# Old state in halves of 64 rows, keys' transposes behind the values' products: a scan of 12 chunks and the two layers behind it

## The chip, the cores and the metric

The kernel runs on one core of a Trainium2 chip. The metric is the device time of one execution in microseconds (us), from the median of several executions. The engines are named as in the profile: PE (TensorE, with PEld for its weight loads), DVE (VectorE), ACT (ScalarE), POOL (GpSimd) and SP, which issues most DMAs.

## The reference, cut to what matters

Three parts run one after the other. The first is a recurrence with a decay w for each head and channel; the second a mixing layer over tokens and then channels; the third sends each token to one of eight experts.

```python
for t in range(S):                                  # S = 768, 8 heads of 48 channels, 2 batches
    cur = einsum('bhd,bhe->bhde', u * kt, vt)
    y[:, :, t] = einsum('bhd,bhde->bhe', rt, state + cur)
    state = w * state + einsum('bhd,bhe->bhde', kt, vt)
x  = y                                              # (2, 768, 384)
u_ = x + (relu(x.T @ w_tok1) @ w_tok2).T            # token mixing
x2 = u_ + relu(u_ @ w_ch1) @ w_ch2                  # channel mixing
...
out[b, s] = p[e] * (relu(x2[b, s] @ w1[e]) @ w2[e]) # e: argmax of x2 @ w_gate, or the token before's
```

## The kernel before, in words

**The scan.** The recurrence is computed in chunks of 128 tokens: 6 chunks for each of 2 batches, so `t` counts 12 chunks. The loop `for t in range(NT)` in `_emit` is one step for each chunk, software-pipelined by hand: step t finishes chunk t and prepares chunks t+1 and t+2. The order of every engine's work is the order in which the code emits it; there is no scheduler. A step emits, for PE: `old(t+1)` (a product with the identity that puts the old state `st` into the PSUM tile `kp`), `scores(t+1)` (keys by queries into two tiles `at`), `pre_ks(t+2)` (four transposes of the scaled keys into `kt`), `beta(t+1)` and `update(t+1)` (both into `kp`), `values(t)` (old state by queries, L431, and masked scores by values, L436, into `y`), `turn(t-1)` (transposes of the result x into `tp`) and products of the token mixing (`mix1`, `mix2`, lines 357 to 359). For DVE: `pre_rk(t+2)` (L372, scales queries and keys by powers of w), `masks(t+1)` (L418), `pre_beta(t+2)` (L377), pieces of the weights' conversion, and `finish(t)`, which reads `y` and writes x (L485). For ACT: the copy of the transposed keys to `ks` (L385), `state(t+1)` (L476, four activations that read `kp` and write the next `st`), the copies of `beta`, eight activations for `bon` (L394), casts and the copies of `tp` (L501). For the first chunk of a batch there is no old state and DVE writes the new one (L480); the last chunk of a batch (t = 5 and 11) needs neither update nor transposed keys. So there are 8 calls of `old` with work in them and 8 of the four activations.

`kp` holds, for two heads at a time, a 128 x 96 block of which only the two 64 x 48 blocks on the diagonal mean anything: rows 0 to 63 with columns 0 to 47, and rows 64 to 127 with columns 48 to 95. The state tiles `sts` are zero elsewhere.

**PSUM tiles in turn.** `ps_tile` hands out five PSUM tiles in turn (`turn_of`, counted by `nps`); whoever gets one must wait until the readers of its last user are done. In the channel mixing's first quarter three of them are accumulators, and two are taken in turn for the products `c1`; behind that, `turn_of` goes back to five.

**Weights' conversion.** The weights arrive as 64-bit numbers. `conv_parts` turns them into a high and a low part in 16 pieces, three calls a piece: DVE scales and masks (L323, L324), joins (L328), joins (L330) and ACT loads the next piece; at the first call of the next piece ACT casts the high part (L291) and POOL subtracts to get the low part (L292). The calls are spread by hand: `CONV_N` in the scan, `CONV_B` in the stretch behind it, and then one list entry of `later` for each `chan_step` of the channel mixing (`work`). A `chan_step(n, f)` is the block f (of 12) for quarter n (of 4): products `ch1` into a tile `c`, ACT's `hh` (L362), DVE's `hl` (L363), and two steps later the products `ch2`. The list `order` weaves quarters 0 and 1: ..., (0, 8), (0, 9), (1, 7), (0, 10), (0, 11), ...

Of the kernel before, what the change touches and what calls it, by code (L numbers as in the profile page):

```python
# [14 lines left out]
ACTF = mybir.ActivationFunctionType  # L15
ALU = mybir.AluOpType
# [6 lines left out]
NCH = S // 128  # L23
NT = B * NCH
# [6 lines left out]
WARM = (6, 12, 3)  # L31
T1 = 4
CONV_N = (0, 2, 2, 3, 2, 3, 2, 2, 2, 2, 1, 0)
CONV_B = (0, 1, 0, 0, 0, 1, 1, -1, 0, 0)
HI_MIN, HI_MAX = (float(x) for x in np.array([0x38100000, 0x47EFFFFF], np.int32).view(np.float32))

# [39 lines left out]
def _emit(ctx, tc, a_in, wu, u_row, wt1, wt2, wc1, wc2, wgl, wex, cst_in, cst_a, out):  # L76
    nc = tc.nc
# [36 lines left out]
    turn_of, nps = [0, 1, 2, 3, 4], [0]  # L114

    def ps_tile(name, shape=(128, 512), k=None):
        if k is None:
            k = turn_of[nps[0] % len(turn_of)]
            nps[0] += 1
        return psw.tile(list(shape), F32, tag=f"w{k}", name=name)  # L120
# [4 lines left out]
    def act(shape, dt, name):  # L125
        return apc.tile(shape, dt, tag=name, name=name)
# [4 lines left out]
    def CA(name):  # L131
        a, b = CSTA[name]
        return cta[:, a:b]
# [4 lines left out]
    def load_a(t, part=None):  # L138
        if t not in a_t:
            rk = ap.tile([128, 1024], F32, tag="rk", name=f"rk{t}", bufs=4)  # L140
            v = ap.tile([128, DM], F32, tag="v", name=f"v{t}", bufs=4)
            a_t[t] = (rk, v)
        for p, (dst, c0) in enumerate(zip(a_t[t], (0, 1536))):
            if part is None or p == part:
                nc.sync.dma_start(out=dst, in_=a_in[t, :, c0:c0 + dst.shape[1]])
# [15 lines left out]
    def warm_up(n):  # L161
        for _ in range(n):
            nc.tensor.matmul(warm_ps, lhsT=warm[:, 0:128], rhs=warm[:, 0:384], start=True, stop=True)
# [43 lines left out]
    for g in range(2):  # L207
        ps = slice(64 * g, 64 * g + 64)
        nc.gpsimd.tensor_tensor(out=uw[ps, :, g], in0=wuc[ps, 4:8], in1=pw[ps, 0], op=ALU.mult)
    w128 = act([128, 4], F32, "w128")  # L210
# [56 lines left out]
    def conv_load():  # L267
        n = nload[0]
        if n >= len(conv) or (n >= 10 and not cpool_):
            return  # L270
        nload[0] += 1
        k, h = conv[n]
        src = wt1 if k == 0 else wt2 if k == 1 else None
        if src is None:
            src = (wc1, wc2)[k % 2][(k - 2) // 2]
        if n < 10:
            raw = rawp.tile([128, 768, 2], I32, tag="raw", name="raw")
        else:
            raw = cpool_[0].tile([128, 768, 2], I32, tag=f"e{n - 10}", name="raw")
        src = src.bitcast(I32)  # L280
        if k > 1 and k % 2 == 0:
            src = src.rearrange("p (c n) -> p c n", c=3)[:, :, h * 512:(h + 1) * 512]
            nc.sync.dma_start(out=raw.rearrange("p (c n) t -> p c (n t)", c=3), in_=src)
        else:
            nc.sync.dma_start(out=raw.rearrange("p n t -> p (n t)"), in_=src[:, h * 1536:(h + 1) * 1536])
        conv_raw.append(raw)
# [65 lines left out]
    def conv_do(n=3):  # L352
        for _ in range(n):
            next(conv_work, None)
# [15 lines left out]
    def pre_rk(t):  # L370
        rk = a_t[t][0]
        nc.vector.tensor_tensor(out=rk, in0=rk, in1=PP.rearrange("p a q j -> p (a q j)"), op=ALU.mult)  # L372
# [6 lines left out]
    def pre_ks(t):  # L379
        rk = a_t[t][0]  # L380
        kt = ps_tile("kt")
        for q in range(4):
            nc.tensor.transpose(kt[:, q * 128:(q + 1) * 128], rk[:, 512 + q * 128:512 + (q + 1) * 128], CA("ident"))
        ks_t[t] = ap.tile([128, 512], F32, tag="ks", name="ks")
        nc.scalar.copy(ks_t[t], kt)  # L385
# [3 lines left out]
    def pre_bonus2(t):  # L389
        beta = ap.tile([128, 8], F32, tag="beta", name="beta")  # L390
        (nc.scalar.copy if t % NCH else nc.vector.tensor_copy)(beta, beta_t.pop(t))
        bon = ap.tile([128, 8, D], F32, tag="bon", name="bon")
        for h in range(8):
            nc.scalar.activation(out=bon[:, h], in_=heads(a_t[t][1])[:, h], func=ACTF.Copy, scale=beta[:, h:h + 1])  # L394
        bon_t[t] = bon

    at_t, ks_t = {}, {}
    kp_t = {}
# [40 lines left out]
    sts = [act([128, 4, 96], F32, f"st{j}") for j in range(3)]  # L439


    def old(t):
        kp = ps_tile("kp")
        kp_t[t] = kp[:, 0:384].rearrange("p (q e) -> p q e", q=4)
        beta_t[t] = kp[:, 384:392]
        if t % NCH in range(1, NCH - 1):
            nc.tensor.matmul(kp_t[t], lhsT=CA("ident"), rhs=sts[(t - 1) % 3], start=True, stop=False)

    def beta(t):
        pp = pp_t.pop(t)  # L450
# [8 lines left out]
    def update(t):  # L459
        ks, v = ks_t.pop(t), a_t[t][1]  # L460
        first = t % NCH == 0
        for h in range(8):
            q, g = divmod(h, 2)
            nc.tensor.matmul(
                kp_t[t][64 * g:64 * g + 64, q, 48 * g:48 * g + 48],
                lhsT=ks[:, h * 64:(h + 1) * 64],
                rhs=v[:, h * D:(h + 1) * D],
                start=first,
                stop=first or q == 3,
            )  # L470

    def state(t):
        kpv = kp_t[t]
        if t % NCH > 0:
            for q in range(4):
                nc.scalar.activation(out=sts[t % 3][:, q], in_=kpv[:, q], func=ACTF.Copy, scale=w128[:, q:q + 1])  # L476
            return
        for g in range(2):
            ps, cs = slice(64 * g, 64 * g + 64), slice(48 * g, 48 * g + 48)
            nc.vector.tensor_tensor(out=sts[t % 3][ps, :, cs], in0=kpv[ps, :, cs], in1=w128[ps].unsqueeze(2).to_broadcast([64, 4, 48]), op=ALU.mult)  # L480

    def finish(t):
        b, c = divmod(t, NCH)
# [92 lines left out]
    for t in range(NT):  # L576
        if t + 3 < NT:
            load_a(t + 3, 0)
        if t == 0:
            conv_load()  # L580
            conv_load()
        grow = t + 1 < NT and (t + 1) % NCH < NCH - 1
        if t + 1 < NT:
            old(t + 1)
            scores(t + 1)
            if t == 0:
                warm_up(WARM[2])
        if t + 2 < NT:
            pre_rk(t + 2)
            if (t + 2) % NCH < NCH - 1:  # L590
                pre_ks(t + 2)
        conv_ahead()
        if t + 1 < NT:
            masks(t + 1)
            beta(t + 1)
        if t + 2 < NT:
            pre_beta(t + 2)
        if grow:
            update(t + 1)
            state(t + 1)  # L600
        values(t)
        if t + 1 < NT:
            pre_bonus2(t + 1)
        if t + 3 < NT:
            load_a(t + 3, 1)
        if t < NT - 1:
            conv_do(CONV_N[t])
        finish(t)
        if t == 0:
            conv_abs(0)  # L610
        if t == NT - 1:
            conv_do(CONV_N[t])
        if t >= 7:
            mix2(*m2.pop(0))
        if t == 10:
            usplit(0)
        if t >= 1:
            turn(t - 1)
            m1.append(t - 1)
            if t >= T1:  # L620
                for _ in range(2):
                    if m1:
                        mix1(m1.pop(0))
# [39 lines left out]
    def ch2(n, f, h):  # L663
        b, half = divmod(n, 2)
        ch, cl = W[f"c2{f // 4}"]
        if f == 0:
            if n == 0:
                turn_of[:] = [0, 1]
            ch_acc[n] = [acc_tile(c) if n else ps_tile("acc", (128, 384), 2 + c) for c in range(3)]
        acc = ch_acc[n]  # L670
        for c in range(3):
            o = (f % 4) * 384 + c * 128
            mm3(acc[c], ch[:, o:o + 128], cl[:, o:o + 128], *h, f == 0, f == 11)
            if f == 11:
                u = xT[b][:, c, half * 384:(half + 1) * 384]
                nc.vector.tensor_tensor(out=u, in0=u, in1=acc[c], op=ALU.add)
        if n == 0 and f == 11:
            turn_of[:] = [0, 1, 2, 3, 4]

    later = []  # L680

# [19 lines left out]

    conv_tail(CONV_B[0])
    turn(11)
    chan_step(0, 0)
    conv_tail(CONV_B[1])
    mix1(11)
    conv_tail(CONV_B[2])
    chan_step(0, 1)
    chan_step(0, 2)
    conv_tail(CONV_B[3])  # L710
    for half in range(2):
        for c in range(3):
            mix2(1, half, c, -1 if half else (2, 0, 1)[c])
            conv_tail(CONV_B[4 + 3 * half + c])
    actx.close()
# [9 lines left out]
    ident = idw[:, 0, 0:128]  # L725
# [493 lines left out]
        for _ in side:  # L1219
            pass  # L1220

    later.extend([lambda j=j: conv_do(2 - j % 2) for j in range(16)])
    later.append(conv_do)
    order = [(0, 3), (1, 0), (1, 1), (1, 2)]
    for f in range(4, 8):
        order += [(0, f), (1, f - 1)]
# [60 lines left out]
    with tc.If(nreg > 0):  # L1287
        with tc.tile_pool(name="ov", bufs=1) as ovp:
# [9 lines left out]
                out=sel, in0=pfx.unsqueeze(1).to_broadcast([128, NOV, 96]), in1=C("ovn").unsqueeze(2).to_broadcast([128, NOV, 96]), op=ALU.is_equal  # L1298
# [91 lines left out]
```

## Time and profile before

| what | before |
|---|---|
| median of 3 executions | 421.62 us (421.58 to 422.22) |
| the profiled execution | 421.5 us, of which 420.0 us are its span |
| PE busy | 397.4 us (95% of the span) |
| DVE, ACT, POOL busy | 274.7, 192.1, 88.4 us |
| granted TensorE clock, mean | 0.987 of full speed |

The scan's loop ends near 100 us; the rest of the token mixing, the channel mixing and the experts follow. The profile's busy share is an average over stages, so the stages are looked at one by one below; a wait is told in brackets behind an instruction, with the engine and line that ended it.

### The profile page before, as it was taken

The numbers are of one execution on the slowest core, as the hardware profiler recorded it, in microseconds if no ns is written. First come the engines' busy times: TensorE is split into PE (matmuls) and PEld (weight loads), VectorE is DVE, ScalarE is ACT, GpSimd is POOL, SyncE is SP. The second block draws the span as 40 slices with busy tenths as digits, with TensorE's granted clock in tenths as the row PEclk, the third lists the DMA queues.
The fourth block names the chain that finished last, engine by engine and source line by source line (L and its number), as shares of the span: only waits on it lengthen the run. The fifth ranks groups of instructions, "written<-read, shape, count | busy, mean of one in ns | idle before, by whom it ended". The sixth has DMA issues, their size and how long they took to land. (4 is left out here: it accounts for less than half of the span.)

```text
span 420.0 us, 8633 instructions
## 1 busy us (share of the span) xinstructions
PE 397.4 (95%) x3348; PEld 378.8 (90%) x3348; DVE 274.7 (65%) x592; ACT 192.1 (46%) x459; POOL 88.4 (21%) x83
## 2 busy tenths in 40 slices
PE   7896987999999998999999999999999999999994
PEld 3685967899999998899999999999999999999994
DVE  6799877775678987447433256759777677675430
ACT  1786566484144333221312121643755665654531
POOL 2016143333122331100000002033241222122110
PEclk9999998999999999999999999999999999999998
DMA  7746462303194000010100013781789867562000
GB/s 259 276 119 224 164 214 90 132 29 108 19 368 159 2 1 0 2 56 2 56 2 1 2 57 104 290 299 28 291 283 419 268 211 247 198 197 89 20 23 14
DMA packets 18336, 55.88 MB, mean 133 GB/s; under 512 B 3921, under 2 KB 7795, under 8 KB 18290
## 3 DMA queue, kind: packets, MB, share of 16 engines
q1 hardware_dynamic: 16370, 49.96, 33.8%
q0 software_dynamic: 1920, 5.32, 4.1%
q8 instruction: 27, 0.44, 0.4%
q14 instruction: 19, 0.16, 0.1%
HBM read 52.31 MB, written 5.91 MB: 139 GB/s over the span
## 5 line engine op out<-in xcount | busy, mean ns | idle before, releaser
L362 ACT ACTIVATE hh<-c 128x384 fp32r<-128x384 f32 x48 | 23.6, 492 | 89.7 <-PE c L359 76.8
L1038 DVE TENSOR_TENSOR we<-wr,we 128x768 fp32r<-128x768 f32 x54 | 51.6, 960 | 15.0 <-ACT we L1037 15.0
L363 DVE SCALAR_TENSOR_TENSOR hl<-c,hh 128x384 fp32r<-128x384 f32 x48 | 26.5, 553 | 40.9 <-ACT hh L362 40.9
L362 ACT ACTIVATE hh<-e 128x256 fp32r<-128x256 f32 (+1 forms) x72 | 25.2, 350 | 57.7 <-PE e L359 45.1
L363 DVE SCALAR_TENSOR_TENSOR hl<-e,hh 128x256 fp32r<-128x256 f32 (+1 forms) x72 | 27.3, 379 | 35.7 <-ACT hh L362 35.6
L357 PE MATMUL acc<-hh,c 128*128 128x384 f32 x144 | 49.6, 344 | 0.0
L358 PE MATMUL acc<-hh,c 128*128 128x384 f32 x144 | 48.4, 336 | 0.2 <-POOL c L292 0.2
L359 PE MATMUL acc<-hl,c 128*128 128x384 f32 x144 | 48.2, 335 | 0.0
L1037 ACT CAST we<-wr 128x768 fp32r<-128x768 f32 x56 | 46.0, 829 | 3.0 <-DMA wr<-in_wex 3.0
L357 PE MATMUL acc<-we,hh 128*128 128x384 f32 x120 | 42.8, 357 | 0.0
L358 PE MATMUL acc<-we,hl 128*128 128x384 f32 x120 | 40.4, 337 | 0.0
L359 PE MATMUL acc<-we,hh 128*128 128x384 f32 x120 | 40.4, 336 | 0.0
L358 PE MATMUL c<-uh,c 128*128 128x384 f32 x108 | 36.3, 336 | 2.1 <-POOL c L292 2.1
L292 POOL TENSOR_TENSOR c<-f,c 128x768 fp32r<-128x768 f32 x12 | 23.0, 1915 | 65.9 <-ACT c L291 65.9
L357 PE MATMUL c<-uh,c 128*128 128x384 f32 x108 | 36.2, 336 | 0.0
L359 PE MATMUL c<-ul,c 128*128 128x384 f32 x108 | 36.1, 335 | 0.0
L358 PEld LDWEIGHTS acc<-hh,c 128*128 128x128 f32 x144 | 27.1, 188 | 0.5 <-POOL c L292 0.5
L357 PE MATMUL e<-gx,we 128*128 128x256 f32 x96 | 27.2, 284 | 0.0
L359 PEld LDWEIGHTS acc<-hl,c 128*128 128x128 f32 x144 | 27.0, 188 | 0.0
L357 PEld LDWEIGHTS acc<-hh,c 128*128 128x128 f32 x144 | 27.0, 188 | 0.0
L359 PE MATMUL e<-gx,we 128*128 128x256 f32 x96 | 27.0, 281 | 0.0
L358 PE MATMUL e<-gx,we 128*128 128x256 f32 x96 | 27.0, 281 | 0.0
(243 smaller groups left out, 977.8 us busy)
## 6 DMA issues: line engine op xcount, KB each, us to landing
wr<-in_wex SPq DMA_DIRECT2D x32, 768.0 KB
raw<-in_wc SPq DMA_DIRECT2D x12, 768.0 KB
rk<-in_a_in SPq DMA_DIRECT2D x12, 512.0 KB
raw<-in_wt SPq DMA_DIRECT2D x4, 768.0 KB
v<-in_a_in SPq DMA_DIRECT2D x12, 192.0 KB
x<-yscr ACTq DMA_DIRECT2D x12, 192.0 KB
xs<-rows SPq DMA_DIRECT2D x8, 192.0 KB
xs<-row SPq DMA_DIRECT2D x4, 192.0 KB
```

The lines of the kernel that those rows point to most:

```text
L292: nc.gpsimd.tensor_tensor(out=ls, in0=f, in1=hs.bitcast(F32), op=ALU.subtract)
L357: nc.tensor.matmul(ps, lhsT=lh, rhs=rh, start=first, stop=False)
L358: nc.tensor.matmul(ps, lhsT=ll, rhs=rh, start=False, stop=False)
L359: nc.tensor.matmul(ps, lhsT=lh, rhs=rl, start=False, stop=last)
L362: nc.scalar.activation(out=hi, in_=ps, func=ACTF.Relu)
L363: nc.vector.scalar_tensor_tensor(out=lo, in0=ps, scalar=0.0, in1=hi.bitcast(F32), op0=ALU.max, op1=ALU.subtract)
L1037: nc.scalar.copy(hi[:, cs], raw[:, cs])
L1038: eng.tensor_tensor(out=lo[:, cs], in0=raw[:, cs], in1=hi[:, cs].bitcast(F32), op=ALU.subtract)
```

## The change

Four edits. `old` now issues two products in place of one: each takes 64 columns of the identity, so that it writes 64 rows of `kp`, and only the 48 columns for each pair of heads that these rows need. `kp` shrinks to 64 x 48 blocks for both halves (192 columns instead of 384), `update` writes there, and `state` reads the halves apart: eight activations of 64 x 48 in place of four of 128 x 96. `pre_ks(t+2)` is emitted behind `values(t)` and `pre_bonus2(t+1)` instead of ahead of `masks(t+1)`. The list of conversion calls in the channel mixing is 2, 1, 2, 1, 2, 1, 2, 1, 2, 2, 2, 2, 1, 2, 1, 1 in place of 2, 1, 2, 1, ... with a last 3. And when the first quarter is done, the turn of five starts with the older of the two tiles that were taken in turn.

```diff
 WARM = (6, 12, 3)
 T1 = 4
 CONV_N = (0, 2, 2, 3, 2, 3, 2, 2, 2, 2, 1, 0)
+CONV_C = (2, 1, 2, 1, 2, 1, 2, 1, 2, 2, 2, 2, 1, 2, 1, 1)
...
     def old(t):
         kp = ps_tile("kp")
-        kp_t[t] = kp[:, 0:384].rearrange("p (q e) -> p q e", q=4)
+        kp_t[t] = kp[:, 0:192].rearrange("p (q e) -> p q e", q=4)
         beta_t[t] = kp[:, 384:392]
         if t % NCH in range(1, NCH - 1):
-            nc.tensor.matmul(kp_t[t], lhsT=CA("ident"), rhs=sts[(t - 1) % 3], start=True, stop=False)
+            for g in range(2):
+                r = slice(64 * g, 64 * g + 64)
+                nc.tensor.matmul(kp_t[t][r], lhsT=CA("ident")[:, r], rhs=sts[(t - 1) % 3][:, :, 48 * g:48 * g + 48], start=True, stop=False)
...
             nc.tensor.matmul(
-                kp_t[t][64 * g:64 * g + 64, q, 48 * g:48 * g + 48],
+                kp_t[t][64 * g:64 * g + 64, q],
...
             for q in range(4):
-                nc.scalar.activation(out=sts[t % 3][:, q], in_=kpv[:, q], func=ACTF.Copy, scale=w128[:, q:q + 1])
+                for g in range(2):
+                    ps = slice(64 * g, 64 * g + 64)
+                    nc.scalar.activation(out=sts[t % 3][ps, q, 48 * g:48 * g + 48], in_=kpv[ps, q], func=ACTF.Copy, scale=w128[ps, q:q + 1])
...
-            nc.vector.tensor_tensor(out=sts[t % 3][ps, :, cs], in0=kpv[ps, :, cs], in1=w128[ps].unsqueeze(2).to_broadcast([64, 4, 48]), op=ALU.mult)
+            nc.vector.tensor_tensor(out=sts[t % 3][ps, :, cs], in0=kpv[ps], in1=w128[ps].unsqueeze(2).to_broadcast([64, 4, 48]), op=ALU.mult)
...
             pre_rk(t + 2)
-            if (t + 2) % NCH < NCH - 1:
-                pre_ks(t + 2)
         conv_ahead()
...
             pre_bonus2(t + 1)
+        if t + 2 < NT and (t + 2) % NCH < NCH - 1:
+            pre_ks(t + 2)
...
         if n == 0 and f == 11:
-            turn_of[:] = [0, 1, 2, 3, 4]
+            a = nps[0] % 2
+            turn_of[:] = [a, 1 - a, 2, 3, 4]
+            nps[0] = 0
...
-    later.extend([lambda j=j: conv_do(2 - j % 2) for j in range(16)])
-    later.append(conv_do)
+    later.extend([lambda j=j: conv_do(j) for j in CONV_C])
```

PE in step 7 of the scan, before the change: `old(8)`, the first two products of `scores(8)`, the keys' transposes of chunk 9, `beta(8)`, `update(8)`, both parts of `values(7)`, and the first product of `mix2`.

```order
L447 MATMUL kp<-st_187,cta 128x384
L406 MATMUL at_1095<-rk_856 128x128
L406 MATMUL at_1096<-rk_856 128x128
...
L383 MATMUL kt<-cta,rk_971 128x128 x4
L455 MATMUL kp<-uw,pp 64x2 x8
L464 MATMUL kp<-v_857,ks 64x48 x8
L431 MATMUL y<-st_186,rk_751 64x96 x8
L436 MATMUL y<-v_752,am_998 64x48 x2
...
L357 MATMUL acc_1194<-t_664,t1h 128x384
```

The same step with the change (line numbers are one to five higher behind the edits):

```order
L450 MATMUL kp<-st_187,cta 64x192 x2
L407 MATMUL at_1121<-rk_876 128x128
L407 MATMUL at_1122<-rk_876 128x128
...
L458 MATMUL kp<-uw,pp 64x2 x8
L467 MATMUL kp<-v_877,ks 64x48 x8
L432 MATMUL y<-st_186,rk_771 64x96 x8
L437 MATMUL y<-v_772,am_1012 64x48 x2
...
L384 MATMUL kt<-cta,rk_991 128x128 x4
L358 MATMUL acc_1224<-t_680,t1h 128x384
```

The transposes stood ahead of `beta`, `update` and `values`; they now stand behind them, next to the mixing's products, and the old state is two products of 64 x 192.

ACT in the same step, before the change: the copy of chunk 9's keys, the magnitude of a piece of weights, the state of chunk 8 and what follows.

```order
L385 COPY ks<-kt 128x512
L315 ACTIVATE f<-raw 128x768
L476 ACTIVATE st_188<-kp,w_184 128x96 x4
L391 COPY beta<-kp 128x8
L394 ACTIVATE bon<-v_857,beta 128x48 x8
```

With the change:

```order
L316 ACTIVATE f<-raw 128x768
L481 ACTIVATE st_188<-kp,w_184 64x48 x8
L392 COPY beta<-kp 128x8
L395 ACTIVATE bon<-v_877,beta 128x48 x8
L386 COPY ks<-kt 128x512
```

The copy of the keys moved from the front to the end, and the state takes eight activations.

DVE in the channel mixing, before the change. The rows `hl` are, in order, the blocks (0, 9), (1, 7), (0, 10); the rows between them are calls of the conversion, and `ul` belongs to the block (0, 11).

```order
L363 SCALAR_TENSOR_TENSOR hl<-c_2136,hh 128x384
L330 SCALAR_TENSOR_TENSOR f<-raw,f 128x768
L363 SCALAR_TENSOR_TENSOR hl<-c_2161,hh 128x384
L323 TENSOR_SCALAR f<-f 128x768
L324 TENSOR_SCALAR f<-f 128x768
L328 SCALAR_TENSOR_TENSOR f<-raw,f 128x768
L363 SCALAR_TENSOR_TENSOR hl<-c_2189,hh 128x384
```

With the change, from the block (0, 8) on:

```order
L364 SCALAR_TENSOR_TENSOR hl<-c_2153,hh 128x384
L331 SCALAR_TENSOR_TENSOR f<-raw,f 128x768
L364 SCALAR_TENSOR_TENSOR hl<-c_2178,hh 128x384
L324 TENSOR_SCALAR f<-f 128x768
L325 TENSOR_SCALAR f<-f 128x768
L329 SCALAR_TENSOR_TENSOR f<-raw,f 128x768
L364 SCALAR_TENSOR_TENSOR hl<-c_2206,hh 128x384
```

The last join of the fifteenth piece stood behind the `hl` of (0, 9); it now stands behind that of (0, 8), and the next piece's start behind (0, 9) instead of (1, 7): one block earlier.

## Rows read from the trace of the kernel before

**Rows 1.** Windows: length, then busy of each engine, clock, DMA share, GB/s

```profile
10.50:105.00 94.50, 84.54 (x1288) 74.57 (x1286) 75.40 (x107) 63.06 (x198) 30.54 (x21) 0.96 0.44 151
105.00:160.00 55.00, 54.79 (x314) 54.47 (x314) 44.41 (x58) 20.23 (x33) 13.60 (x8) 1.00 0.29 105
160.00:186.00 26.00, 23.16 (x138) 21.84 (x138) 13.01 (x30) 8.00 (x17) 3.76 (x2) 1.00 0.07 23
```

**Rows 2.** Waits of PE from 9 to 100 us: total, times, longest

```profile
PE kt L383 <- DVE rk L372: 7.8, 4, 4.0
```

**Rows 3.** Windows with the columns of rows 1, around two stretches of the scan

```profile
37.10:40.50 3.40, 0.76 (x12) 0.63 (x12) 3.37 (x6) 2.21 (x7) 2.10 (x1) 1.00 0.71 217
40.50:44.00 3.50, 3.50 (x64) 3.50 (x60) 3.46 (x4) 2.71 (x9) 2.19 (x2) 0.51 0.56 219
67.80:71.30 3.50, 3.50 (x61) 3.41 (x57) 2.19 (x4) 3.47 (x14) 0.00 (x0) 0.51 0.21 63
```

**Rows 4.** Timeline of PE in step 9: start, duration, instruction

```profile
81.33 0.81 PE L447 MATMUL kp<-st,cta 128*128 128x384 f32 x2
82.07 1.16 PE L406 MATMUL at<-rk 64*128 64x128 f32 x16
83.16 0.63 PE L455 MATMUL kp<-uw,pp 128*64 128x2 f32 x16
83.65 0.65 PE L464 MATMUL kp<-v,ks 128*64 128x48 f32 x16
84.13 0.85 PE L431 MATMUL y<-st,rk 128*64 128x96 f32 x16
84.81 1.09 PE L436 MATMUL y<-v,am 128*64 128x48 f32 x32
85.83 0.44 PE L357 MATMUL acc<-t,t1h 128*128 128x384 f32 x1
```

**Rows 5.** Timeline of PE in step 7, and the start of step 8

```profile
62.95 1.16 PE L406 MATMUL at<-rk 64*128 64x128 f32 x16
66.44 0.63 PE L383 MATMUL kt<-cta,rk 128*128 128x128 f32 x4 [2.32 <-DVE rk L372]
66.99 0.63 PE L455 MATMUL kp<-uw,pp 128*64 128x2 f32 x16
...
71.20 0.44 PE L357 MATMUL acc<-t,t1h 128*128 128x384 f32 x1
...
74.47 1.16 PE L406 MATMUL at<-rk 64*128 64x128 f32 x16
```

**Rows 6.** Timeline of DVE in steps 5 to 7

```profile
47.83 1.29 DVE L418 TENSOR_TENSOR am<-at,cst 128x512 f32<-128x512 f32 x2 [1.73 <-PE at L406]
...
64.51 1.78 DVE L372 TENSOR_TENSOR rk<-rk,PP 128x1024 f32<-128x1024 f32 x1
...
71.31 0.56 DVE L485 TENSOR_TENSOR x<-y,bon 128x384 f32<-128x384 f32 x1 [1.29 <-PE y L436]
```

**Rows 7.** Timeline of ACT in the scan

```profile
22.09 1.04 ACT L476 ACTIVATE st<-kp,w 128x96 f32<-128x96 f32 x4 [0.20 <-PE kp L464]
...
35.68 1.91 ACT L394 ACTIVATE bon<-v,beta 128x48 f32<-128x48 f32 x8
```

**Rows 8.** Windows of ACT alone: length, busy, clock, DMA share, GB/s

```profile
27.00:32.50 5.50, 5.47 (x18) 1.00 0.51 163
```

**Rows 9.** Timeline of all engines in the channel mixing

```profile
157.31 0.49 ACT L362 ACTIVATE hh<-c 128x384 fp32r<-128x384 f32 x1 [1.91 <-PE c L359]
...
160.82 0.83 ACT L291 CAST c<-f 128x768 fp32r<-128x768 f32 x1
...
161.72 1.92 POOL L292 TENSOR_TENSOR c<-f,c 128x768 fp32r<-128x768 f32 x1 [4.27 <-ACT c L291]
...
163.69 0.44 PE L358 MATMUL c<-uh,c 128*128 128x384 f32 x1 [1.55 <-POOL c L292]
...
177.35 0.44 PE L357 MATMUL c<-ue,c 128*128 128x384 f32 x1 [0.58 <-DVE xT L676]
```

## The prediction

> **What bounds the kernel now.** I looked first at the windows by stage [rows 1]. From 105 to 160 us PE is busy 54.79 of 55.00 us: nothing but fewer or faster products shortens that. In the scan, 10.5 to 105 us, it is busy 84.54 of 94.50 us with a mean clock of 0.96, and from 160 to 186 us 23.16 of 26.00. So time can be had in two places, some 10 us of idle PE in the scan (and what the slow clock costs there) and 2.8 us in the channel mixing. Second, the waits of PE in the scan [rows 2]: 7.8 us, in 4 waits, are the keys' transposes standing until DVE has scaled the keys two chunks ahead. Third, the clock [rows 3]: after a stretch in which PE did 0.76 us of work in 3.4, the granted clock is 0.51, that is 1.2 GHz for 2.4, for about 3.5 us, and again from 67.8 to 71.3 us. Each such stretch does 1.7 us of work in 3.5. Fourth, the timelines of single steps: step 9, in which PE waits for nothing [rows 4], and step 7, in which it waits 2.32 us at the transposes and then runs its values at the low clock [rows 5]. Last, the channel mixing, where single waits of PE can be read.
>
> **The wait at the keys' transposes.** In step 7 PE starts its scores at 62.95 and the mixing's product, behind the values, at 71.20: 8.25 us [rows 5]. The same work at full clock, from step 9 [rows 4]: scores 83.16 - 82.07 = 1.09, beta 0.49, update 0.48, values 0.68 + 1.02; and the transposes 0.55 from step 7 itself (66.99 - 66.44). Sum 4.31. With the transposes last, PE reaches them at 62.95 + 3.76 = 66.71; DVE's scaled keys are there at 64.51 + 1.78 = 66.29 [rows 6]. So beta, update and values hide the wait, 0.4 us to spare; without that cover 2.32 us come back. Nothing then idles ahead of the values, and I take them at full clock. Step 7 gives 8.25 - 4.31 = 3.9 us to PE.
>
> **What is late next.** The tiles in turn come in the order kp, at, at, y, kt, tp instead of kp, at, at, kt, y, tp. Six are handed out a step and there are five, so each takes the tile of the fifth before it: the second `at` of chunk t+1 now gets that of y(t-1), and scores(t+1) must wait until DVE has written x(t-1). (Before, the transposes had that tile and that wait.) Behind the scores on PE stand beta, update, values and the transposes; ACT's state and DVE's masks wait for them. x(7) was held 1.29 us by the values [rows 6]; free of that it starts at 70.02 and ends at 70.6. PE would reach the scores of step 8 at 67.26 plus what lies between 71.20 and 74.47 before, 3.27 less 0.2 for the cheaper old state, so at 70.3. It waits 0.3 us and starts them at 70.6, against 74.47: 3.9 us earlier.
>
> **Steps 1 to 6.** Here DVE has little idle time, and what it waits for PE is what can be won: 1.73 us in step 5 [rows 6], which goes if the scores of step 6 no longer stand behind step 4's late transposes. Against it stands ACT: the state takes eight activations. Four of 128 x 96 take 1.04 us [rows 7]; eight of 128 x 48 (bon) 1.91. The length of a row hardly counts, so eight of 64 x 48 are near 1.9: 0.87 us more in each of 8 steps, 7.0 us of ACT. In most of the scan ACT has room (63.06 of 94.50 [rows 1]), but from 27.0 to 32.5 us it is busy 5.47 of 5.50 us [rows 8], and there the state, the beta behind it, and the copy of the keys, now behind both, come later; PE's update waits for that copy. If 0.87 is paid in each of steps 1 to 3 that is 2.6 us; if the new order of the queue hides it, nothing. DVE has slack of its own, so I take 0.6. Sum for steps 1 to 6: 1.73 - 0.6 = 1.1 us won, between -0.9 and 1.7.
>
> **The old state.** Before, 81.33 to 82.07: 0.74 us [rows 4]. The state's part of the values shows products of 64 columns that run in pairs: 8 products of 96 elements in 0.68 us, 0.17 a pair. Two products of 192 elements are one pair: 0.34 if all of it scales, 0.17 if none does. I take 0.34, since twice the elements have to pass, and 0.1 for one more change of shape ahead of it: 0.44 to 0.5. The change of shape is bounded by the values: 16 products of 48 take 1.02 us to the next 128-wide product, twice the update's 8 (0.48) is 0.96, so 0.06 of it is the change. The gain is 0.2 to 0.3 us a step where PE is the bound: step 8's is in the 3.9 above, step 9 adds 0.25. The transposes, now next to other 128-wide products, save one change of shape, under 0.1 us. Sum 0.3. The Trainium skill, TensorEngine Tiling (Array Packing), Key Properties, speaks against this edit: changing the tiling mode drains the engine, and the split puts one more such change into each step. The trace shows a change, at 0.06 us; by a drain as long as a whole product of the old state lasts the gain of 0.25 would shrink to nothing, and the sum below by 0.3 us.
>
> **The channel mixing.** At 163.69 PE has waited 1.55 us for POOL's low part of the weights for block (0, 10) [rows 9]. POOL started at 161.72, behind ACT's cast at 160.82, which stands behind the `hh` of (1, 7). With the new list the cast stands behind the `hh` of (0, 9), which came at 157.31: the cast can run from 157.8 to 158.6, POOL end near 160.5, and PE wants it at 162.1 (163.69 less 1.55). The cost: in the six blocks before, DVE makes ten calls of the conversion instead of nine. A block is 18 products, 3.14 us of PE by 314 products in 54.79 us, and DVE's share of it is 2.54 (44.41 of 55.00) [rows 1]. One call more, at most 1.7 us with 1.5 calls a block, fits into six times 0.6 us, and `hl` has two blocks of slack. So 1.55 goes. At 177.35 PE waits 0.58 us for DVE to have read an accumulator whose tile is next in turn; starting with the older of the two tiles avoids it. Together 2.1 us. Both waits of rows 9 could also come back elsewhere; then nothing is won here.
>
> **Sum.** 3.9 + 1.1 + 0.3 + 2.1 = 7.4 us. The stages behind the scan are bound by PE or move with it, so I let all of it reach the end: 420.0 - 7.4 = 412.6 us of span, and with the 1.5 us that lie around the span in the profiled execution (421.5), 414.1 us. That execution stands 0.1 us from the median of 421.62, so I predict 414 us.
>
> **The rivals.** (a) The clock still falls in steps 4 and 5, since DVE's scaling of chunk 6 comes no earlier and PE must stand somewhere: 1.73 stays lost there and the low clock lasts into the next step's mixing. For it: the deepest wait is in that place [rows 2, 3] and none of its causes on DVE is removed. 414.1 + 1.7 = 415.8. (b) The new wait of the scores for x paces every step from 5 on, so the scan wins only what DVE waited for, 1.73 + 1.29 - 0.6 = 2.4 in place of 5.3: 417.0. Against it: DVE is busy 75.40 of 94.50 us. (c) The calls of the conversion are late on DVE and the wait at 163.69 only moves: 415.7. (d) The columns don't run in pairs, so the split does not do what it says: 0.74 + 0.1 instead of 0.44, 0.3 in each of steps 7 to 9: 415.0. (e) The other side: ACT. The state's end holds back the next old state, and with it the scores, the masks and everything else of a step. If all 7.0 us lie on the path, and eat the scan's gains too, the time is 421.5 + 7.0 - 2.1 = 426.4. It decides from the point where the state ends later than PE has finished values, transposes and `tp`, which is 1.70 + 0.55 + 0.25 = 2.5 us (0.25 an estimate from the transposes, three of four) behind the update, with 1.9 of it needed: for that ACT must be 0.6 us behind with its queue. From 27 to 32.5 us it may be [rows 8]; behind step 6 the mixing's products add cover.
>
> **How the numbers follow.** My forecast (412 to 415) has 0.45; (a) 0.20; (b) 0.12; (c) 0.08; (d) 0.08; (e) 0.07. The range of 8 in 10 takes in (a) to (d) and, below, steps 1 to 6 without ACT's loss and waits that I haven't counted (the old state in steps 1 to 6): 411.3 to 418.0. A measurement of this kernel tells 0.2%, 0.8 us, from no change. All cases but (e) are faster by more; a mild form of (e) that cancels the gains is the middle: faster 0.92, same 0.02, slower 0.06.
>
> **What would show it.** Right: no wait of PE at the transposes in step 7, values of step 7 at the full clock, products of the old state of which two start within a few ns, a gap of about 0.45 us between the old state's start and the scores; state activations of 0.23 us each in eights; short waits of the scores for L485's x; no wait for POOL at the block (0, 10). Wrong: PE standing at the old state for ACT, a stretch of the low clock near 44 us, the wait for POOL at another block.

## The result, and the profile after

The changed kernel takes 417.83 us (median of 4 runs, 417.82 to 418.31); the kernel before, run beside it, 421.92 us (421.58 to 422.63). The ratio is 0.9904, with an interval of 0.9887 to 0.9921. The forecast of 414.0 had the sign right and its range (411.3 to 418.0) held by 0.2 us. Of the 7.4 us that it promised 4.1 came; the traces show 3.2 of span, all of it from the channel mixing, which was to give 2.1.

The page's busy times of the changed kernel, which answer to the table of the section on the profile before:

```profile
span 416.8 us, 8706 instructions
...
PE 395.2 (95%) x3364; PEld 378.6 (91%) x3364; DVE 277.6 (67%) x592; ACT 202.9 (49%) x491; POOL 87.6 (21%) x83
```

The windows by stage (columns of rows 1): the scan, the end of the channel mixing's first quarter, and two stretches at the low clock:

```profile
10.50:102.00 91.50, 81.70 (x1291) 72.30 (x1290) 75.20 (x104) 71.52 (x226) 27.75 (x20) 0.96 0.44 150
157.00:183.00 26.00, 25.46 (x157) 25.15 (x156) 15.00 (x32) 8.60 (x18) 3.69 (x2) 1.00 0.07 23
21.50:25.00 3.50, 3.50 (x62) 3.50 (x64) 3.43 (x5) 3.40 (x10) 1.00 (x1) 0.52 0.11 13
42.00:45.50 3.50, 3.50 (x50) 3.24 (x46) 3.50 (x5) 2.36 (x6) 2.44 (x2) 0.52 0.92 370
```

Against rows 1, ACT does 71.52 us of work in the scan instead of 63.06, and in 26 us of channel mixing PE is busy 25.46 instead of 23.16. The work that ran at 1.2 GHz from 67.8 to 71.3 us [rows 3] runs at full clock now; a stretch at 21.5 us has come in its place. Both traces have two such stretches of 3.4 us, so the clock does not set them apart.

The waits of PE from 9 to 100 us show where the wait of 7.8 us at the transposes [rows 2] went:

```profile
PE tp L505 <- ACT beta L392: 4.6, 4, 2.2
PE kp L458 <- ACT beta L392: 2.2, 1, 2.2
PE kp L450 <- issue: 1.3, 1, 1.3
PE y L432 <- DVE x L490: 0.7, 1, 0.7
PE kt L384 <- DVE rk L373: 0.3, 1, 0.3
```

The transposes wait 0.3 us. PE waits 4.6 + 2.2 = 6.8 us for ACT's copy of beta instead. Before, it waited for that copy once:

```profile
PE tp L500 <- ACT beta L391: 0.5, 1, 0.5
```

The 1.3 us at the old state (L450), for which the view names no engine, are likely ACT's as well: PE goes on at 19.03, 0.09 behind the end of the copy of beta, which stands behind the eight activations; before the change it went on at 18.35, 0.10 behind the same copy.

```profile
18.77 0.17 ACT L392 COPY beta<-kp 128x8 f32<-128x8 f32 x1
```

PE's timeline shows what these waits do to the steps:

```profile
40.37 0.63 PE L458 MATMUL kp<-uw,pp 128*64 128x2 f32 x16 [2.20 <-ACT beta L392]
...
63.60 0.55 PE L450 MATMUL kp<-st,cta 128*64 128x192 f32 x4
64.07 1.16 PE L407 MATMUL at<-rk 64*128 64x128 f32 x16
...
72.36 1.16 PE L407 MATMUL at<-rk 64*128 64x128 f32 x14 [0.17 <-DVE x L490]
...
80.06 0.55 PE L505 MATMUL tp<-cta,x 128*128 128x128 f32 x3 [2.24 <-ACT beta L392]
...
82.06 1.16 PE L407 MATMUL at<-rk 64*128 64x128 f32 x16
```

Take the starts of the scores as marks. Step 7's come at 64.07 instead of 62.95 [rows 5]: steps 1 to 6 have lost 1.1 us. Step 7 itself lasts 72.36 - 64.07 = 8.29 us instead of 74.47 - 62.95 = 11.52: 3.2 won. Step 8 lasts 82.06 - 72.36 = 9.70 instead of 82.07 - 74.47 = 7.60: 2.1 lost. At step 9 the two kernels stand at 82.06 and 82.07 [rows 4]: the scan has won nothing.

ACT's timeline shows the queue in which beta stands, first the head of the queue in step 4, then step 8:

```profile
36.89 0.92 ACT L316 ACTIVATE f<-raw 128x768 f32<-128x768 f32 x1 [1.19 <-POOL t L293]
...
76.59 0.93 ACT L316 ACTIVATE f<-raw 128x768 f32<-128x768 f32 x1 [3.14 <-DMA raw<-in_wc]
77.40 2.43 ACT L481 ACTIVATE st<-kp,w 64x48 f32<-64x48 f32 x8
79.84 0.17 ACT L392 COPY beta<-kp 128x8 f32<-128x8 f32 x1
```

In step 8 the magnitude `f` waits 3.14 us for a piece of weights, the state behind it takes 2.43 us, and only then comes beta, for which PE's transposes of x (80.06) have waited 2.24 us: they take the next tile in turn, which is that of `kp`, and it is released only when beta has been read from it. All of the 3.2 us of span come behind the scan. The timeline of the channel mixing (hh is the nonlinearity that closes a block; rows 9 hold some of before):

```profile
157.30 0.49 ACT L363 ACTIVATE hh<-c 128x384 fp32r<-128x384 f32 x1 [1.83 <-PE c L360]
157.91 0.84 ACT L292 CAST c<-f 128x768 fp32r<-128x768 f32 x1
158.82 1.85 POOL L293 TENSOR_TENSOR c<-f,c 128x768 fp32r<-128x768 f32 x1 [3.69 <-ACT c L292]
160.41 0.49 ACT L363 ACTIVATE hh<-c 128x384 fp32r<-128x384 f32 x1 [1.67 <-PE c L360]
...
161.73 0.33 PE L358 MATMUL c<-uh,c 128*128 128x384 f32 x1
161.90 0.33 PE L359 MATMUL c<-uh,c 128*128 128x384 f32 x1
...
163.54 0.49 ACT L363 ACTIVATE hh<-c 128x384 fp32r<-128x384 f32 x1 [2.64 <-PE c L360]
```

POOL starts at 158.82 instead of 161.72. The first product of the block (0, 10) starts at 161.73 (161.74 before); the second, which needs POOL's low part, follows at 161.90 without a wait, instead of at 163.69. The `hh` of before, from the same view of its trace, stand at 160.43, 165.47, 168.77, 171.70, 175.29 and 183.80; those of after at 160.41, 163.54, 166.86, 169.78, 172.85 and 180.56. The changed kernel's lead is 0.0 us, then 1.9 for three blocks, 2.4, and 3.2 from the turn of the tiles on, and it stays so to the end (span 416.8 for 420.0).

### The profile page after: what moved, and what is told of

Its sections match the earlier page's. It is cut to its first block, busy times and chain, and to the rows that moved or that the text cites. A ratio compares the mean times of both kernels' runs of the same rounds, so it can differ in the third digit from the quotient of the medians.

```text
span 416.8 us, 8706 instructions
## 1 busy us (share of the span) xinstructions
PE 395.2 (95%) x3364; PEld 378.6 (91%) x3364; DVE 277.6 (67%) x592; ACT 202.9 (49%) x491; POOL 87.6 (21%) x83
```

## The experiments

Two questions were open. Why did the scan win nothing: did ACT's eight small activations take back what the transposes' new place gives, or was that place worth little, whatever ACT does, since the waits go elsewhere (the late piece of weights, x, the clock)? And is the split of the old state worth anything by itself? On the two chips of the runs the kernel before took 424.24 and 424.31 us (17 runs each), so ratios to it are compared, and 1% is 4.2 us. The intervals behind the ratios leave about 2 to 2.6 us of doubt in a difference of two of them. Expectations in us are meant beside 421.92 us: a ratio times that is the time to hold against them.

**The channel mixing alone.** The kernel before with `CONV_C` and the new `turn_of`, nothing of the scan's edits.

> The kernel before with only the new list of conversion calls and the new turn of tiles; the scan is untouched. Theory A (the scan's edits give and take the same, the whole gain lies in the channel mixing): 421.9 less the 3.2 us by which the two traces differ behind the scan, 418.5 to 419. Rival (the scan's edits do win, and the conversion list only moves a wait): 420.5 or more.

Measured: 420.2 us, 0.9903 (0.9865 to 0.9941), the ratio of the whole change; beside 421.92 us that is 417.8, a little below theory A and far from the rival. PE waits 7.8 us at the transposes, as before. The scan's edits together are worth nothing that can be measured.

**Only the transposes' new place, with the channel mixing.** Old state, `kp` and the state's activations as before:

```diff
-            for g in range(2):
-                r = slice(64 * g, 64 * g + 64)
-                nc.tensor.matmul(kp_t[t][r], lhsT=CA("ident")[:, r], rhs=sts[(t - 1) % 3][:, :, 48 * g:48 * g + 48], start=True, stop=False)
+            nc.tensor.matmul(kp_t[t], lhsT=CA("ident"), rhs=sts[(t - 1) % 3], start=True, stop=False)
...
-                for g in range(2):
-                    ps = slice(64 * g, 64 * g + 64)
-                    nc.scalar.activation(out=sts[t % 3][ps, q, 48 * g:48 * g + 48], in_=kpv[ps, q], func=ACTF.Copy, scale=w128[ps, q:q + 1])
+                nc.scalar.activation(out=sts[t % 3][:, q], in_=kpv[:, q], func=ACTF.Copy, scale=w128[:, q:q + 1])
```

> The changed kernel with the old state's product, the update and the state's four activations as before; the keys' transposes stay behind the values and the tail edits stay. Theory A (eight activations of 64 rows, 2.45 us against 1.04, hold up beta, the kp tile and the next old state): faster than the changed kernel, 415 to 416.5, and the waits of PE for the beta copy shrink from 6.8 us to under 3. Theory B (the pieces of weights arrive late and set the scan's pace, whatever the state costs): within 0.8 us of the changed kernel, 417 to 418.5.

Measured: 413.05 us, 0.9744 (0.9702 to 0.9787). The waits of PE from 9 to 105 us, and ACT's timeline at the step that answers to the rows of step 8 above:

```profile
PE y L432 <- DVE x L486: 2.0, 1, 2.0
...
PE tp L501 <- ACT beta L392: 0.7, 2, 0.4
```

```profile
72.41 0.95 ACT L316 ACTIVATE f<-raw 128x768 f32<-128x768 f32 x1 [2.77 <-DMA raw<-in_wc]
73.23 1.02 ACT L477 ACTIVATE st<-kp,w 128x96 f32<-128x96 f32 x4
```

The piece of weights is as late as in the changed kernel (2.77 us for 3.14), yet PE waits 0.7 us for beta and not 6.8: with a state of 1.02 us the queue behind `f` is short enough. Against the kernel with the channel mixing alone the transposes' place is worth 0.9903 - 0.9744 = 1.6%, 6.7 us, give or take 2.4. The clock is not the reason: the traces of both kernels have 6.8 us at 1.2 GHz. Beside 421.92 us the ratio makes 411.1, faster than theory A's 415 to 416.5.

**Only the halves, with the channel mixing.** `pre_ks(t + 2)` goes back behind `pre_rk(t + 2)`, the rest is the change.

> The changed kernel with the keys' transposes back ahead of the masks; the split of the old state and the tail edits stay. Theory A: it keeps ACT's cost and loses the cover for the transposes' wait, so it is slower than the changed kernel and than the tail edits alone, 419 to 421. Theory B: 418 to 419.

Measured: 426.28 us, 1.0038 (1.001 to 1.0067): slower than before, and 1.35%, 5.7 us (give or take 2.0), slower than the channel mixing alone. Beside 421.92 us that is 423.5, worse than both theories. PE's waits from 9 to 105 us and the windows of three stretches:

```profile
PE kt L384 <- DVE rk L373: 6.5, 3, 4.2
PE tp L505 <- ACT beta L392: 3.2, 4, 1.4
PE kp L450 <- issue: 1.9, 1, 1.9
```

```profile
20.10:27.00 6.90, 6.90 (x90) 6.35 (x92) 3.88 (x6) 5.06 (x16) 1.01 (x1) 0.51 0.01 2
44.00:50.80 6.80, 5.92 (x72) 5.53 (x73) 6.65 (x8) 5.25 (x16) 3.22 (x2) 0.50 0.51 202
64.50:71.30 6.80, 5.54 (x50) 5.38 (x46) 2.62 (x5) 6.32 (x21) 1.06 (x1) 0.50 0.44 163
```

The old wait stays, the wait for beta comes on top, and three stretches of some 6.8 us run at 1.2 GHz: 20.5 us at the low clock, for 6.8 in the trace of the channel mixing alone. At half the speed the 13.7 us more can cost up to 6.8 us, so here the loss need not be ACT's queue alone; how it splits between the waits and the clock, this run does not tell. The two edits of the scan are thus large and of opposite signs: -6.7 us and, on either kernel, +5.7 to +6.8 (0.9744 to the change's 0.9904, taken on another chip, is 1.6%, 6.8 us, give or take 1.9).

**The state's rows in order.** All four activations of rows 0 to 63 first, then those of rows 64 to 127:

```diff
-            for q in range(4):
-                for g in range(2):
+            for g in range(2):
+                for q in range(4):
```

> The changed kernel with the eight activations of the state ordered by halves: four on rows 0 to 63, then four on rows 64 to 127. If the 0.31 us between them comes from changing the half each time: 0.23 us in seven of eight, the state in 1.9 us, and the time 0.5 to 1.5 us shorter. If it belongs to an activation of 64 rows: 0.31 us again, same time as the changed kernel within 0.4 us.

Measured: 416.36 us, 0.9816 (0.9772 to 0.9859). The groups of the state's activations, first in the changed kernel, then in this one; then one eight of this one's timeline:

```profile
L481 ACT ACTIVATE st<-kp,w 64x48 f32<-64x48 f32 x64 | 18.9, 295 | 2.5 <-PE kp L467 1.8
```

```profile
L481 ACT ACTIVATE st<-kp,w 64x48 f32<-64x48 f32 x64 | 13.7, 288 | 2.6 <-PE kp L467 2.5
...
66.19 1.71 ACT L481 ACTIVATE st<-kp,w 64x48 f32<-64x48 f32 x8
```

One activation is as long (288 and 295 ns), but in order of rows they overlap more: an eight takes 1.71 us instead of 2.45. From start to start it is 0.19 us on the same half and 0.30 at the one change of half, against 0.31 throughout. PE's waits for beta fall from 6.8 us to 3.1, and the time by 0.9%, 3.7 us (give or take 2.0), more than the 0.5 to 1.5 expected. The 32 activations of before take 8.2 us in all. The changed kernel's 10.7 us more cost 6.8, so 0.6 of what is added to ACT's state reaches the end (0.5 to 0.8 by the intervals). This kernel's 5.5 more cost 0.9816 - 0.9744 = 0.7%, 3.0 us; that agrees, but with 2.6 us of doubt it shows little by itself.

**The state on DVE.** The changed kernel with `if False:` for `if t % NCH > 0:` in `state`, so that DVE's two products of `state` do every chunk.

> The changed kernel with every state written by DVE in its two products of 64 x 192 (0.72 us, the form that it has for a batch's first chunk) instead of eight activations. Theory A (only ACT's queue spoils the scan): the split of the old state then costs nothing and pays 0.25 us a step, so the kernel is as fast as the one with the four activations, ratio 0.970 to 0.980 to the kernel before. Rival (DVE, which scales, masks and converts, is the next bound): its 8 x 0.72 us come back on the path, ratio 0.982 to 0.992.

Measured: 417.39 us, 0.9835 (0.9796 to 0.9873). The scan's window and PE's waits from 9 to 105 us:

```profile
10.50:100.00 89.50, 82.81 (x1290) 73.12 (x1289) 77.66 (x120) 53.67 (x162) 28.04 (x20) 0.94 0.46 157
```

```profile
PE tp L505 <- ACT beta L392: 3.0, 3, 1.4
PE y L432 <- DVE x L490: 1.5, 1, 1.5
PE at L407 <- DVE x L490: 1.1, 1, 1.1
```

ACT falls to 53.67 us, DVE rises to 77.66 of 89.50, and PE now waits 2.6 us for x. Most of the 3.0 us for ACT's copy of beta are DVE's too, for in two of these three places (2.3 us) the copy itself waits for the state from DVE (2.63 us at 60.52, and 3.59 at 70.31):

```profile
70.31 0.17 ACT L392 COPY beta<-kp 128x8 f32<-128x8 f32 x1 [3.59 <-DVE st L485]
```

So DVE is the next bound, as the rival had it. If four activations (0.9744) are the measure, it gives back 0.9%, 3.8 us (give or take 2.4), of the 6.8 that ACT's relief brings.

**Does the split pay once ACT is out of it?** The kernel with only the transposes' place and the channel mixing, the state on DVE.

> The version with the old state's whole product and the keys' transposes behind the values, with every state written by DVE. Against the run with the split and the state on DVE it shows what the split itself is worth once ACT is out of it: by the rows 0.25 us in each of 8 steps, of which those on the path count, 0.5 to 2 us in favour of the split. If the split is worth nothing on PE: the two within 0.5 us.

Measured: 416.11 us, 0.9821 (0.9783 to 0.986), beside 0.9835 with the split: the same, 0.6 us apart the wrong way, give or take 2.3. The gain of 0.5 us or more that was expected of the split does not show, but one of up to 1.7 us is not ruled out.

**An earlier piece of weights.** The kernel with the transposes' place and the channel mixing, and a third buffer for the raw weights, so that the piece on which `f` waits is loaded a piece earlier:

```diff
-            raw = rawp.tile([128, 768, 2], I32, tag="raw", name="raw")
+            raw = (apc if n in (2, 5) else rawp).tile([128, 768, 2], I32, tag="raw", name="raw")
...
-            conv_load()
+            if n != 5:
+                conv_load()
...
+        if t == 1:
+            conv_load()
```

> The version with four activations, and a third buffer for the pieces of weights during the scan: pieces 2 and 5 lie in it, and every load of a piece is issued one piece earlier. ACT's wait of 2.8 us for a piece in step 8 is then gone. If the late piece sets the pace there (what is left of theory B): 1 to 2 us faster than with two buffers, ratio 0.969 to 0.973. If PE and DVE have enough other work: same ratio, 0.9744, within 0.003.

Measured: 412.24 us, 0.9732 (0.9706 to 0.9757). ACT's timeline at the same place:

```profile
68.05 0.94 ACT L316 ACTIVATE f<-raw 128x768 f32<-128x768 f32 x1 [0.22 <-POOL c L293]
```

The wait of 2.77 us is gone, and the time is the same as without the buffer (0.9744) within the intervals: 0.5 us less, give or take 2.1. In the traces step 8 lasts 7.87 us for 8.35. So the late piece costs about half a microsecond by itself; with a state of 2.43 us behind it, step 8 of the changed kernel was 2.1 us longer than before.

**The list of conversion calls alone.** The kernel before with `CONV_C` only.

> The kernel before with only the new list of conversion calls. By the traces its part is 1.9 us at the block (0, 10) and 0.5 us behind it, and the turn of tiles has the other 0.8 us: ratio 0.994 to 0.995. If the list and the turn need each other: 0.997 or more.

Measured: 421.42 us, 0.993 (0.9899 to 0.9961). By these ratios the list carries most of the channel mixing's gain; whether the turn of the tiles adds the 0.8 us that the trace shows lies within the intervals (0.3%, give or take 0.5%, and on two chips).

## Why the prediction was right in its range and wrong in its terms

- **The wait at the transposes: right.** 3.9 us forecast for step 7, 3.2 in the trace. The wait went, but for the 0.3 us by which DVE's keys came later than forecast; the values ran at full clock, and the scores' new wait for x is 0.17 us. With the channel mixing, this edit alone reaches 0.9744, 6.7 us beyond the channel mixing; forecast for the step and for what DVE had to win were 3.9 + 1.7. In that kernel's trace step 7 lasts 68.18 - 60.66 = 7.5 us, 4.0 less than before. Rival (b), 2.4 us for the scan, falls with that: x holds the scores 0.3 us there, and the values of step 4 once, 2.0.
- **ACT's state: the step that failed.** "Eight of 64 x 48 are near 1.9" was taken from `bon` [rows 7]; they took 2.45. `bon`'s eight work on all 128 rows, each of these on the other half of the rows than the one before it. So the state adds 1.4 us to a step instead of 0.87, and the 0.6 us that the sum took for it became 6.8 on the path, of 10.7 us more on ACT: the term was eleven times too small.
- **Its place, and the path.** The forecast put it at 27.0 to 32.5 us, where ACT is full. The longest waits came at 40.37 (2.20 us) and 80.06 (2.24 us), where ACT has idle time on average but its queue is held: at 36.89 `f` has waited 1.19 us for POOL, at 76.59 it has waited 3.14 us for a late transfer. Rival (e) had the mechanism but the deciding point wrong: it counted `tp` as work that covers the state. By the prediction's own rule of the fifth tile before, `tp` takes the tile of `kp` and cannot start until beta has been read behind the state, as the rows at 79.84 and 80.06 show. The cover is thus 1.70 + 0.55 = 2.25 us, and by these rows state and beta (2.45 and 0.17) exceed it even when ACT is not behind; in steps from 7 on, the products of `mix2` cover some more.
- **That the range held is luck.** Its upper end took in (a) to (d), and none of these happened at its price. For the scan the mild form of (e) happened, a cost that cancels the gains, which got 2 in 100. That a gain of 6.7 us and a loss of 6.8 met, and that the channel mixing gave a microsecond more, put the time 0.2 us inside.
- **Rival (a), the clock.** The low stretch at 42 us stayed and another came at 21.5; the one of step 7 went. So the clock fell where (a) said, but its price of 1.7 us does not explain the time: the kernel with the transposes' place alone also has 0.96 in its scan, has 6.8 us at 1.2 GHz around 42 us and DVE's wait at the masks of step 5 (1.85 us, 1.73 before), and is 6.8 us faster than the changed one.
- **The old state: right in size, without effect.** From 63.60 to 64.07 is 0.47 us, forecast 0.44 to 0.5, against 0.74 [rows 4]: the columns run in pairs (two of the four records start 6 or 7 ns apart), and rival (d) falls. The change of shape behind the pair costs 0.05 us (0.25 from the last record's start to the scores, 0.21 between the two pairs), not the length of a product. A saving of 0.27 us a step does not show in the time; the runs leave room for 1.7 us in all.
- **The channel mixing: right in both places, too small.** 3.2 us instead of 2.1. A wait's idle time was counted (1.55 and 0.58), but PE loses more than that: product records of 0.33 us follow each other 0.17 apart, and idle time starts only at the end of the last record. The second product of the block started at 163.69 before and at 161.90 now, 1.8 us apart, and the products behind the wait followed a little slower, which makes the 1.9. Half a microsecond more came at the next piece of the same chain: it held PE 0.17 us by idle time at 171.95 before and none after, and 171.45 to 171.95 is 0.50 from start to start where 0.17 is usual. By the same count 0.58 became 0.8. Rival (c) falls.
- **The sum** gave 412.6 us of span, and 416.8 came, 4.2 more: the scan's three terms, 3.9 + 1.1 + 0.3 = 5.3 us, came to nothing, and the channel mixing gave 1.1 more.

The version that the runs point to is the one without the halves: 0.9744, or 0.9732 with the third buffer, which these runs do not tell apart.

## What to carry to other kernels

When an edit makes one engine's work cheaper by splitting it, count the instructions that the split adds on the engine that reads the result, and price them by rows of the same shape and the same rows of the tile, not by their number alone. An engine with a fifth of its time idle (ACT: 71.52 busy of 91.50) can still set the pace where an instruction at the head of its queue waits for something late; look at what stands behind each such wait, and at whose buffer it releases. And where several edits are made at once, time each by itself: here a gain of 6.7 us and a loss of about the same size hid each other.

## What the runs showed of the hardware

- Activations of 64 x 48 that alternate between rows 0 to 63 and 64 to 127 start 0.31 us apart and take 0.295 each; on the same half they start 0.19 us apart, with 0.288 each, and 0.30 where the half changes. Only the order was changed between the two. Why the alternation costs 0.1 us, no run shows.
- The old state in halves (four records of 64 columns and 192 elements) takes 0.47 us to the next shape's product, where the whole one (two records of 128 columns and 384 elements) took 0.74 [rows 4].
- The stretches at 1.2 GHz can differ between kernels that run the same scan. The kernel before and the one with the channel mixing alone run the same scan, with the same 7.8 us of waits at the transposes. The first has two stretches of 3.4 us [rows 3], the second, on another chip, one of 6.8 us and none in step 7:

```profile
40.00:46.80 6.80, 6.80 (x77) 6.41 (x76) 6.14 (x7) 4.37 (x13) 3.44 (x3) 0.51 0.45 171
```

In both, the first stretch follows a wait of 3.95 us at the transposes. Over the ten traces, 3.4 to 20.5 us of the first 108 us run at 1.2 GHz, in stretches of 3.4 or 6.8 us, so times of single steps from two traces can differ by the clock alone.
